# A SwiGLU layer on one core: the second quarter-chunk of x is loaded by rows and transposed by TensorE

## The chip, the core and the metric

The kernel runs on one core of one Trainium2 chip. The metric is the device time of one execution in microseconds. The kernel before takes 115.9 us, the median of three runs (115.56, 115.90 and 116.58).

## The reference

```
B, S, D, F = 1, 2048, 512, 1376          # all bf16
def reference(x, w_gate, w_up, w_down):
    g = silu(x @ w_gate)                 # (S, D) @ (D, F)
    u = x @ w_up
    return (g * u) @ w_down              # (S, F) @ (F, D)
```

## The kernel before, in words

The product of gate and up wants D, the contracted dimension, on the partitions, so x is held transposed in `xT_sb` (128 partitions, KD = 4 blocks of D, 2048 tokens). Tokens come in four chunks of 512 (`SC`). Half of the first chunk, `HT` = 256 tokens, is a unit of its own in this change. The weights of gate and up come in slabs of two feature tiles of 128 (`wg0`, `wu0`, then `wg2`, `wu2` and so on) into `w_sb`; w_down comes later into `wd_sb`.

The program is a list of operations (`Plan`). TensorE (P) and SyncE (S, which issues the loads) run theirs in the order in which they were added. ScalarE (A), VectorE (D) and GpSimd (G) get theirs from `schedule`, which takes at each step the operation that could start first by a table of estimated durations and landing times (`land`), and at equal starts the one with the lower priority number. `emit` then puts in the semaphore waits. Operations that read a key wait for its last writer; those that write one wait for its readers too. A key `("b", i)` is PSUM bank i.

The loads in order on SyncE's queue: `xn` (tokens 0 to 255, by rows: partition p holds tokens 2p and 2p + 1), `wg0`, `x0b` (tokens 256 to 511 by a transposing DMA, `load_x`, straight into `xT_sb`), `wu0`, the slab 2 of gate and of up, `x1a` and `x1b` (tokens 512 to 1023, transposing), slabs 4 and 8, `x2`, `x3`, slab 6, w_down and its pieces.

TensorE's start: `warm` (6 matmuls of 512 columns and 2 small ones on constants), then the transposes of `xn` by a product with `ident`, for each of the four blocks dk of D: for dk 0 to 2 four transposes of 64 x 64-row pieces into two banks (L373), for dk 3 four half-width ones into bank 6 (L380). After each dk the piece is copied from PSUM to `xT_sb` (`copy_op`), dk 0 and 2 by VectorE (L326), dk 1 and 3 by ScalarE (L325). Then `between`: N_BETWEEN = 5 pairs of small matmuls on constants into bank 7 (L397), whose result nobody reads. Then the gates of feature tiles 0 and 1 (L424 through `gu_emit`): first on columns 0 to 255, dk by dk as the copies come, then on columns 256 to 511, which wait for `x0b`. Then the ups of both tiles on all 512 columns, which wait for `wu0`. These use pairs of 64-column matmuls side by side in the array.

Behind that, in TensorE's fixed order: feature tiles 2 and 3 of chunk 0, three feature tiles of chunk 1 (all still L424), the products for the last 96 features (`plan_x` L488, `plan_y` L514), and then the main part: Strassen-Winograd units (seven products in place of eight on 2 x 2 blocks) in fp32 for gate and up, whose operands are sums that GpSimd builds from the weights (`w_sums`) and VectorE or GpSimd from x (`x_sums`). The down product is made in part in the same way, in part directly (L720, L748, L858, L870).

Loading by rows leaves the tokens of `xn` in another order in `xT_sb` (position 128 i + p holds token 2p + i). The order is undone where the output is stored: `put` stores tokens 0 to 255 (`fa`) with the pattern `(p j) d` and the rest of chunk 0 with `(j p) d`.

The lines the change touches around the gates are

```
for dk in range(KD):
    for ft, b in ((0, g0), (1, g1)):
        pe(gu_emit(0, ft, 0, b, [dk], 0, HT), [("x0a", dk), wkey[0]], [("b", b)], 0.5)
for ft, b in ((0, g0), (1, g1)):
    pe(gu_emit(0, ft, 0, b, range(KD), HT, SC), ["x0b", wkey[0]], [("b", b)], 2)
```

Of the kernel before, what the change touches and what calls it, by code (L numbers as in the profile page):

```python
# [6 lines left out]
BF16 = mybir.dt.bfloat16  # L7
# [2 lines left out]

N_WARM = 6
N_FILL = 1
N_BETWEEN = 5

PE_STEP, PE_STEP4, PE_LAG = 216, 231, 205
A_BUSY, A_LAG = 485, 180
# [152 lines left out]
def bass_standalone__swiglu_ffn__prompt_kernel(nc, x, w_gate, w_up, w_down, out):  # L169
    _, S, D = x.shape  # L170
    F = w_gate.shape[1]
    P = 128
    KD = D // P
# [4 lines left out]
    SC = 512  # L178
    NSC = S // SC
    TPC = SC // P  # L180
# [4 lines left out]
    HT = SC // 2  # L185
    HC = P // 2
    NXN = HT // P
    NB = 8
# [4 lines left out]
    xf = x[0]  # L193
    of = out[0]
# [4 lines left out]
    with ExitStack() as es:  # L199
        sb = lambda name, shape, dt: es.enter_context(nc.sbuf_tensor(name, shape, dt))  # L200
# [3 lines left out]
        xT_sb = sb("xT_sb", [P, KD, S], BF16)  # L204
# [22 lines left out]
        psum = ps("psum", [P, NB, 512], FP32)  # L227
        turn = [0, 2, 1, 3, 4, 5, 6, 7]
        bank = lambda i: psum[:, i, :]

        xn_sb = sb("xn_sb", [P, NXN, D], BF16)
        ident = sb("ident", [P, P], BF16)
        diag = sb("diag", [P, P], mybir.dt.int32)

# [6 lines left out]
            rest.remove(i)  # L241
            return i

        homes = dict(xn=14, x0b=22, wg0=30, x0c=13, wu0=21, wg2=29, wu2=20, wg4=12, wu4=28, wg6=19)

        ones_w = nc.const_aps.tensor(1.0, [P, P], BF16)
        ones_m = nc.const_aps.tensor(1.0, [P, SC], BF16)
# [29 lines left out]
        def load_x(name, t0, t1):  # L277
            load(
                name, lambda e: e.dma_start_transpose(xT_sb[:, :, t0:t1], xf[t0:t1, :]), [name], 1500, 4 * (t1 - t0)  # L279
            )  # L280

        load(
            "xn",
            lambda e: e.dma_start(  # L284
                xn_sb[:, :, :].rearrange("p j d -> p (j d)"), xf[0:HT, :].rearrange("(p j) d -> p (j d)", j=NXN)
            ),
            ["xn"], 500, 770,
        )
# [33 lines left out]
        def copy_op(engs, out, src, reads, writes, prio, busy=None, after=()):  # L322
            def emit(e):
                if e is engines["A"]:
                    return e.activation(out, src, ACT.Copy)  # L325
                return e.tensor_copy(out, src)  # L326
            b = A_BUSY if engs == "A" else D_BUSY
            return plan.add(engs, emit, reads, writes, busy or b, A_LAG if engs == "A" else D_LAG, prio, after=after)
# [16 lines left out]
        def pe(emit, reads, writes, n, step=PE_STEP, after=()):  # L345
            return plan.add("P", emit, reads, writes, int(n * step), PE_LAG, dma=None, after=after)
# [17 lines left out]
        def tview_last():  # L364
            return psum[:, 6, 0:P].bitcast(BF16).rearrange("p (i t) -> p i t", i=NXN)

        def transposes(dk):
            def emit(e):
                for i in range(NXN):
                    if dk < KD - 1:  # L370
                        for h in range(2):
                            t0 = h * HC
                            ins = e.transpose(  # L373
                                tview(dk)[:, h, i, :], xn_sb[t0:t0 + HC, i, dk * P:(dk + 1) * P],
                                ident[t0:t0 + HC, t0:t0 + HC],
                            )
                    else:
                        for m in (0, HC):
                            c0 = dk * P + m
                            ins = e.transpose(tview_last()[m:m + HC, i, :], xn_sb[:, i, c0:c0 + HC], ident[:, :])  # L380
                return ins
            return emit

        for dk in range(KD):
            keys = [("b", 2 * dk), ("b", 2 * dk + 1)] if dk < KD - 1 else [("b", 6)]
            pe(transposes(dk), ["xn", "ident"], keys, 0.5)
            out, src = xT_sb[:, dk, 0:HT], tview_last()
            if dk < KD - 1:
                out, src = out.rearrange("p (i h t) -> p h i t", i=NXN, h=2), tview(dk)
            else:  # L390
                out = out.rearrange("p (i t) -> p i t", i=NXN)
            copy_op("DA"[dk % 2], out, src, keys, [("x0a", dk)], 0, 300)

        def between(e):
            for i in range(N_BETWEEN):
# [4 lines left out]
                    )  # L400
            return ins

        pe(between, (), [("b", NB - 1)], N_BETWEEN / 4)

        n_group = 0

# [6 lines left out]
        def x_keys(c):  # L413
            if c == 1:
                return ["x1a", "x1b"]
            if c:
                return [f"x{c}"]
            return [("x0a", dk) for dk in range(KD)] + ["x0b"]

        def gu_emit(m, ft, c, b, dks, n0, n1):  # L420
            def emit(e):
                for dk in dks:
                    for h in (0, HC):
                        ins = e.matmul(  # L424
                            psum[h:h + HC, b, n0:n1], lhsT=w_sb[:, dk, m, ft * P + h:ft * P + h + HC],
                            rhs=xT_sb[:, dk, c * SC + n0:c * SC + n1], start=(dk == 0), stop=(dk == KD - 1),
                            tile_position=(0, h),
                        )
                return ins
            return emit  # L430
# [417 lines left out]
        class DownUnit:  # L848
# [82 lines left out]
            def put(self, c):  # L931
                d0 = 2 * self.q
                reads = [("fin", d, c) for d in (d0, d0 + 1)]
                c0, c1 = d0 * P, (d0 + 2) * P
                if c == 0:
                    store(f"fa{d0}", "A", of[0:HT, c0:c1].rearrange("(p j) d -> p j d", j=NXN), fin_sb[:, 0:NXN, c0:c1], reads)
                t0 = NXN if c == 0 else TPC
                t1 = (c + 1) * TPC
                store(f"f{c}{d0}", "A", of[t0 * P:t1 * P, c0:c1].rearrange("(j p) d -> p j d", p=P), fin_sb[:, t0:t1, c0:c1], reads)

        def last_rest(c0, c1, b):
            t, ob = LAST_T, LAST_T - NST // 2
# [144 lines left out]
```

## Time and profile before

| | us |
|---|---|
| median of three runs (lowest to highest) | 115.9 (115.56 to 116.58) |
| the profiled execution, its own time | 115.87 |
| its span in the profile | 114.5 |
| TensorE matmul busy | 110.8 (97%) |
| VectorE busy | 76.8 (67%) |
| ScalarE busy | 63.7 (56%) |
| GpSimd busy | 61.5 (54%) |
| HBM read | 4.75 MB |

The profile shows one execution. PE is TensorE's matmuls, PEld its weight loads, DVE VectorE, ACT ScalarE, POOL GpSimd, SPq SyncE's queue, where a row's length is the time to issue a DMA, not to move it. L with a number is a line of the kernel. In a row of the timeline the first number is the start from the beginning of the span, the second the length, in us; x with a number counts instructions, and the bracket gives the idle time before and what ended it. Matmul ends are modelled and contain the way through the array, so neighbouring matmuls overlap in their rows, and their rate is read from their starts.

### The profile page before, as it was taken

What the parts mean: (1) busy time and instruction counts of PE and PEld (TensorE: products, weight loads), DVE (VectorE), ACT (ScalarE), POOL (GpSimd) and SP (SyncE); (2) the same over time, 40 slices, a digit from 0 to 9 for tenths busy, and PEclk for the clock granted to TensorE, in tenths of its full rate; (3) what the DMA queues carried; (4) which work ended last, traced back from release to release, by engine and by line L of the source; (5) the groups of instructions that cost most, each with busy time, mean ns of one, the idle gap of its engine ahead of it and who ended that gap; (6) DMA issues with size and microseconds to landing.
All of it is one profiled execution on the core that took longest, in us unless ns stands there. A gap on an engine that the chain in (4) does not pass through costs nothing.

```text
span 114.5 us, 1775 instructions
## 1 busy us (share of the span) xinstructions
PE 110.8 (97%) x652; PEld 69.6 (61%) x660; DVE 76.8 (67%) x113; ACT 63.7 (56%) x123; POOL 61.5 (54%) x57
## 2 busy tenths in 40 slices
PE   7999999999999999999999999999999999999993
PEld 2755566556675857677676858654344557866452
DVE  0113999783966849493958768499999957486423
ACT  5344665865779897767678786740567960000000
POOL 1049103999999999977999989965000000000000
DMA  3999999994000000000000000000031002227876
GB/s 88 265 242 219 325 210 220 273 370 100 0 0 0 3 0 3 0 0 6 0 0 0 3 0 0 0 0 0 13 130 46 0 0 46 52 46 183 195 202 199
DMA packets 22808, 9.84 MB, mean 86 GB/s; under 512 B 12848, under 2 KB 22672, under 8 KB 22800
## 3 DMA queue, kind: packets, MB, share of 16 engines
q1 hardware_dynamic: 20656, 8.69, 31.5%
q10 hardware_dynamic: 2144, 1.05, 3.3%
q8 instruction: 5, 0.08, 0.3%
q14 instruction: 3, 0.02, 0.1%
HBM read 4.75 MB, written 2.10 MB: 60 GB/s over the span
## 4 chain that ended last, share of the span: by engine, by line
PE 91%; DMA 4%; SPq 2%; issue 1%; DVE 1%
PE psum L610 32%; PE psum L720 15%; PE psum L622 12%; PE psum L858 10%; PE psum L424 9%; PE psum L870 4%; DMA w_sb<-in_w_up_dram 4%; PE psum L488 3%; PE psum L748 3%; PE psum L435 2%; PE psum L514 2%; SPq L279 1%; DVE o_sb L326 1%; SPq L267 0%; SPq L284 0%
## 5 line engine op out<-in xcount | busy, mean ns | idle before, releaser
L610 PE MATMUL psum<-tt_sb,ss_sb 128*128 128x512 f32 x160 | 40.1, 404 | 0.0
L610 PEld LDWEIGHTS psum<-tt_sb,ss_sb 128*128 128x128 f32 x160 | 29.9, 188 | 7.6 <-DVE h_sb L337 0.3
L337 DVE TENSOR_TENSOR ts_sb<-r_sb,psum 128x512 f32<-128x512 f32 x32 | 20.6, 681 | 14.8 <-ACT r_sb L325 14.8
L337 POOL TENSOR_TENSOR h_sb<-sg_sb,ts_sb 128x512 bf16<-128x512 f32 x16 | 20.8, 1301 | 2.9 <-ACT sg_sb L332 2.9
L337 DVE TENSOR_TENSOR h_sb<-sg_sb,psum 128x512 bf16<-128x512 f32 x24 | 16.4, 682 | 6.2 <-PE psum L424 5.8
L325 ACT ACTIVATE r_sb<-psum 128x512 f32<-128x512 f32 x32 | 17.3, 596 | 5.5 <-PE psum L610 5.5
L332 ACT ACTIVATE sg_sb<-psum 128x512 f32<-128x512 f32 x24 | 14.3, 600 | 10.6 <-PE psum L610 5.4
L337 POOL TENSOR_TENSOR ss_sb<-w_sb 128x512 fp32r<-128x512 bf16 x10 | 11.4, 1159 | 13.6 <-DVE tt_sb L337 7.1
L720 PE MATMUL psum<-wd_sb,h_sb 128*128 128x512 bf16 (+2 forms) x98 | 17.9, 336 | 0.2 <-issue 0.2
L622 PE MATMUL psum<-xT_sb,w_sb 128*128 128x512 bf16 x59 | 14.2, 380 | 0.4 <-issue 0.2
L720 PEld LDWEIGHTS psum<-wd_sb,h_sb 128*128 128x128 bf16 x100 | 8.2, 98 | 9.2 <-issue 1.0
L424 PE MATMUL psum<-xT_sb,w_sb 128*64 128x512 bf16 (+1 forms) x128 | 12.7, 354 | 0.2 <-DMA w_sb<-in_w_up_dram 0.2
L332 ACT ACTIVATE sg_sb<-ts_sb 128x512 f32<-128x512 f32 x16 | 10.2, 636 | 2.3 <-DVE ts_sb L337 2.3
L424 PEld LDWEIGHTS psum<-xT_sb,w_sb 128*64 128x64 bf16 x128 | 7.7, 112 | 4.8 <-DMA w_sb<-in_w_up_dram 0.5
L622 PEld LDWEIGHTS psum<-xT_sb,w_sb 128*128 128x128 bf16 x64 | 5.5, 98 | 8.0 <-issue 2.5
L326 DVE COPY psum<-psum 128x512 f32<-128x512 f32 x8 | 5.6, 699 | 0.8 <-PE psum L622 0.2
L337 POOL TENSOR_TENSOR ss_sb<-w_sb,ss_sb 128x512 fp32r<-128x512 bf16 x5 | 5.8, 1169 | 0.2
L337 POOL TENSOR_TENSOR ss_sb<-ss_sb,w_sb 128x512 fp32r<-128x512 f32 x5 | 5.8, 1165 | 0.0
L326 DVE CAST o_sb<-psum 128x512 bf16<-128x512 f32 (+2 forms) x6 | 2.9, 512 | 4.2 <-PE psum L720 3.1
L337 POOL TENSOR_TENSOR ss_sb<-wd_sb 128x640 fp32r<-128x640 bf16 x4 | 5.6, 1409 | 0.0
L858 PE MATMUL psum<-tt_sb,ss_sb 128*128 128x512 f32 x20 | 5.6, 417 | 0.0
L858 PE MATMUL psum<-th_sb,ss_sb 128*128 128x512 f32 x20 | 5.5, 413 | 0.0
(72 smaller groups left out, 122.3 us busy)
## 6 DMA issues: line engine op xcount, KB each, us to landing
wd_sb<-in_w_down_dram SPq DMA_DIRECT2D x1, 1280.0 KB, 8.3
w_sb<-in_w_gate_dram SPq DMA_DIRECT2D x4, 256.0 KB, 4.0
w_sb<-in_w_up_dram SPq DMA_DIRECT2D x4, 256.0 KB, 4.2
out_dram<-o_sb SPq DMA_DIRECT2D x7, 128.0 KB, 1.8
out_dram<-xT_sb ACTq DMA_DIRECT2D x4, 128.0 KB, 2.3
out_dram<-xT_sb ACTq DMA_DIRECT2D x2, 256.0 KB, 3.3
w_sb<-in_w_gate_dram SPq DMA_DIRECT2D x1, 352.0 KB, 5.0
w_sb<-in_w_up_dram SPq DMA_DIRECT2D x1, 320.0 KB, 5.5
```

The source lines that it names most:

```text
L325: return e.activation(out, src, ACT.Copy)
L326: return e.tensor_copy(out, src)
L332: "A", lambda e: e.activation(out, src, ACT.Silu), reads, writes, busy, A_LAG, prio
L337: engs, lambda e: e.tensor_tensor(out, a, b, alu), reads, writes, busy,
L424: ins = e.matmul(psum[h:h + HC, b, n0:n1], lhsT=w_sb[:, dk, m, ft * P + h:ft * P + h + HC], rhs=xT_sb[:, dk, c * SC + n0:c * SC + n1], sta ...
L488: ins = e.matmul(psum[m:m + HC, b, :], lhsT=w_sb[:, dk, 0, XC0 + m:XC0 + m + HC], rhs=xT_sb[:, dk, c * SC:(c + 1) * SC], start=(dk == 0), ...
L610: ins = e.matmul(bank(dst), lhsT=s[:, k, :], rhs=t[:, k, :], start=(start and k == 0), stop=(k == KH - 1), skip_group_check=True,)
L622: ins = e.matmul(bank(dst), lhsT=w_sb[:, k0 + k, m, f:f + P], rhs=xT_sb[:, k0 + k, c:c + SC], start=(start and k == 0), stop=(k == KH - 1) ...
L720: ins = e.matmul(psum[:, b, 0:c1 - c0], lhsT=hrows(F_ORDER[n], t, 0, P), rhs=wd_sb[:, F_ORDER[n], c0:c1], start=(start and n == n0), stop= ...
L748: ins = e.matmul(bank(b), lhsT=lhsT, rhs=rhs, start=(start and n == 0), stop=(n == 2 and (kind == "T" or not start)), tile_position=(r0, 0 ...
L858: ins = e.matmul(bank(dst), lhsT=self.ds[s][:, j, self.q, :], rhs=self.dt[t][:, j, :], start=(start and n == 0), stop=(n == NFF // 2 - 1), ...
L870: ins = e.matmul(bank(dst), lhsT=wd_sb[:, 2 * j + a, d * P:(d + 1) * P], rhs=h0_sb[:, 2 * j + a, 0:SC], start=(n == 0), stop=(n == NFF // ...
```

## The change

Tokens 256 to 511 are no longer loaded by the transposing DMA `x0b` but by rows into a second tile, `xn1`, issued as the second load, right behind `xn0` (the old `xn`). TensorE transposes them as it does the first 256: 16 more transposes, four more copies (two on VectorE, two on ScalarE), the last block into bank 7 in place of 6. `between` moves between the two halves and has 3 pairs in place of 5. The gates of tiles 0 and 1 run on all 512 columns at once, dk by dk, and wait for the copies of both halves. The stores of chunk 0 use the pattern `(p j) d` for both halves.

```
-N_BETWEEN = 5
+N_BETWEEN = 3
...
-        xn_sb = sb("xn_sb", [P, NXN, D], BF16)
+        xn_sb = [sb(f"xn_sb{i}", [P, NXN, D], BF16) for i in range(2)]
...
+        def load_xn(i):
+            load(
+                f"xn{i}",
+                lambda e: e.dma_start(
+                    xn_sb[i][:, :, :].rearrange("p j d -> p (j d)"),
+                    xf[i * HT:(i + 1) * HT, :].rearrange("(p j) d -> p (j d)", j=NXN),
+                ),
+                [f"xn{i}"], 500, 770,
+            )
+
+        load_xn(0)
+        load_xn(1)
         load_w("wg0", w_gate, 0, 0, 0, slabs[0][1] * P)
-        load_x("x0b", HT, SC)
         load_w("wu0", w_up, 1, 0, 0, slabs[0][1] * P)
...
+        for half, last in enumerate((6, 7)):
+            if half:
+                pe(between, (), [("b", NB - 1)], N_BETWEEN / 4)
+            for dk in range(KD):
+                keys = [("b", 2 * dk), ("b", 2 * dk + 1)] if dk < KD - 1 else [("b", last)]
+                pe(transposes(half, dk, last), [f"xn{half}", "ident"], keys, 0.5)
+                out, src = xT_sb[:, dk, half * HT:(half + 1) * HT], tview_last(last)
...
+                copy_op("DA"[dk % 2], out, src, keys, [("x0", half, dk)], 0, 300)
...
         for dk in range(KD):
             for ft, b in ((0, g0), (1, g1)):
-                pe(gu_emit(0, ft, 0, b, [dk], 0, HT), [("x0a", dk), wkey[0]], [("b", b)], 0.5)
-        for ft, b in ((0, g0), (1, g1)):
-            pe(gu_emit(0, ft, 0, b, range(KD), HT, SC), ["x0b", wkey[0]], [("b", b)], 2)
+                pe(gu_emit(0, ft, 0, b, [dk], 0, SC), [("x0", 0, dk), ("x0", 1, dk), wkey[0]], [("b", b)], 1)
...
                 if c == 0:
-                    store(f"fa{d0}", "A", of[0:HT, c0:c1].rearrange("(p j) d -> p j d", j=NXN), fin_sb[:, 0:NXN, c0:c1], reads)
...
+                    for i in range(2):
+                        store(
+                            f"f{i}a{d0}", "A", of[i * HT:(i + 1) * HT, c0:c1].rearrange("(p j) d -> p j d", j=NXN),
+                            fin_sb[:, i * NXN:(i + 1) * NXN, c0:c1], reads,
+                        )
```

More of the change, by code (lines that the diff above doesn't have):

```diff
@@ L242, in take @@
             return i
-        homes = dict(xn=14, x0b=22, wg0=30, x0c=13, wu0=21, wg2=29, wu2=20, wg4=12, wu4=28, wg6=19)
+        homes = dict(xn0=14, xn1=22, wg0=30, x0c=13, wu0=21, wg2=29, wu2=20, wg4=12, wu4=28, wg6=19)
         ones_w = nc.const_aps.tensor(1.0, [P, P], BF16)
@@ L362, in tview, with tview_last, transposes @@
             return psum[:, 2 * dk:2 * dk + 2, 0:HC].bitcast(BF16).rearrange("p h (i t) -> p h i t", i=NXN)
-        def tview_last():
-            return psum[:, 6, 0:P].bitcast(BF16).rearrange("p (i t) -> p i t", i=NXN)
-        def transposes(dk):
+        def tview_last(b):
+            return psum[:, b, 0:P].bitcast(BF16).rearrange("p (i t) -> p i t", i=NXN)
+        def transposes(half, dk, last):
             def emit(e):
@@ L373, in emit @@
                             ins = e.transpose(
[L374 removed]
+                                tview(dk)[:, h, i, :], xn_sb[half][t0:t0 + HC, i, dk * P:(dk + 1) * P],
                                 ident[t0:t0 + HC, t0:t0 + HC],
@@ L379, in emit @@
                             c0 = dk * P + m
-                            ins = e.transpose(tview_last()[m:m + HC, i, :], xn_sb[:, i, c0:c0 + HC], ident[:, :])
+                            ins = e.transpose(tview_last(last)[m:m + HC, i, :], xn_sb[half][:, i, c0:c0 + HC], ident[:, :])
                 return ins
             return emit
[L384 to L392, printed above, removed]
         def between(e):
@@ L417, in x_keys @@
                 return [f"x{c}"]
-            return [("x0a", dk) for dk in range(KD)] + ["x0b"]
+            return [("x0", half, dk) for half in range(2) for dk in range(KD)]
         def gu_emit(m, ft, c, b, dks, n0, n1):
```

17 lines of the change are left out of this document (6 added, 11 removed).

## The prediction

> **What bounds the kernel now.** I read the chain of work that ended last first, by line and in order of time, because its pieces say which engine every microsecond of the end depends on.
>
> ```profile
> span 114.5 us, 1775 instructions
> PE 91%; DMA 4%; SPq 2%; issue 1%; DVE 1%
> 1.67 1.33 SPq L279
> ...
> 3.04 4.01 DMA w_sb<-in_w_up_dram
> 7.05 0.04 issue
> 7.10 10.71 PE psum L424 x96
> 17.80 1.73 PE psum L488 x16
> ...
> 104.92 6.82 PE psum L720 x34
> 111.74 0.18 PE psum L945
> ```
>
> From 7.10 us to 111.9 the chain is TensorE almost without a break; ahead of it stand SP's issues and the landing of the first up slab (wu0) at 3.04 + 4.01 = 7.05. So whatever lets the up groups start earlier comes off the end one for one, and nothing else does unless it removes a gap from TensorE's row. One quantity to carry along: 16 matmuls of 64 columns on 512 take 1.73, so 0.108 each, 0.216 a pair.
>
> Second, the start in order of time, TensorE and the two engines that copy out of PSUM. The columns are start, length, engine, line, what, count.
>
> ```profile
> 0.77 2.72 PE L350 MATMUL psum<-const-bfloat16-1.0 128*128 128x512 bf16 x6 [0.77 <-PEq L1072]
> 3.71 0.50 PE L373 MATMUL psum<-ident,xn_sb 64*128 64x64 bf16 x12
> 4.14 0.43 PE L380 MATMUL psum<-ident,xn_sb 128*64 128x128 bf16 x4
> 4.35 0.75 PE L397 MATMUL psum<-const-bfloat16-1.0 128*64 128x128 bf16 x10
> 4.88 1.98 PE L424 MATMUL psum<-xT_sb,w_sb 128*64 128x256 bf16 x32
> 7.10 10.71 PE L424 MATMUL psum<-xT_sb,w_sb 128*64 128x512 bf16 x96 [0.23 <-DMA w_sb<-in_w_up_dram]
> 4.03 0.51 DVE L326 COPY xT_sb<-psum 128x256 bf16<-128x256 bf16 x2 [2.71 <-PE psum L373]
> 4.14 0.85 ACT L325 ACTIVATE xT_sb<-psum 128x256 bf16<-128x256 bf16 x2 [1.91 <-PE psum L373]
> ```
>
> A length ends with a pipeline tail, so I reckon in starts. Transposes of one half: 3.71 to 4.35, **0.64**. Filler: ten matmuls from 4.35 to 4.88, so 0.106 a pair. Gates: 16 pairs of 256 columns from 4.88, at 0.110 a pair (half of 0.216 and a little), leave the array free at 6.64; the ups come at 7.10. Here lie **0.46 us** in which TensorE could take work (the profile calls 0.23 of it idle, the rest is the tail of the last matmuls).
>
> Third, the transfers: SP's issues, and the time from issue to landing of each by windows around its issue.
>
> ```profile
> 0.74 0.40 SPq L284 DMA_DIRECT2D xn_sb<-in_x_dram  x1
> 1.21 0.41 SPq L267 DMA_DIRECT2D w_sb<-in_w_gate_dram  x1
> 1.67 1.33 SPq L279 DMA_TRANSPOSE xT_sb<-in_x_dram  x1
> 3.04 0.57 SPq L267 DMA_DIRECT2D w_sb<-in_w_up_dram  x1
> 7.24 1.51 SPq L279 DMA_TRANSPOSE xT_sb<-in_x_dram  x1
> xn_sb<-in_x_dram SPq DMA_DIRECT2D x1, 256.0 KB, 2.8
> w_sb<-in_w_gate_dram SPq DMA_DIRECT2D x1, 256.0 KB, 3.2
> xT_sb<-in_x_dram SPq DMA_TRANSPOSE x1, 3.9
> xT_sb<-in_x_dram SPq DMA_TRANSPOSE x1, 5.1
> ```
>
> xn lands at 0.74 + 2.8 = 3.54, wg0 at 1.21 + 3.2 = 4.41, x0b (the transposing load, 3.9) at 5.57, wu0 at 7.05. The row with 5.1 is x1b, the second half of tokens 512-1023, issued at 7.24: it lands at 12.34.
>
> **The change part by part.**
>
> *SP's queue.* The 1.33 us issue of x0b goes, a plain load of x by rows (xn1) takes its place one position further forward, at the 0.40 of xn. Issues: xn0 0.74, xn1 1.21, wg0 1.67, wu0 2.14, and so 3.04 - 2.14 = 0.90 earlier for wu0 and for everything behind it (second slabs, x1a, x1b, and on).
>
> *Landings.* xn0 as now, 3.54. xn1 stands where wg0 stood, has its 256 KB, and comes in rows of 2 KB in place of pieces of 512 B, so 4.41 is its upper end; the lower is xn0's own, 3.54, as the two are neighbours. I take 4.41, as no row shows a transfer in second place sooner. For wg0, now third, the ends are 4.41 (its old place) and 5.57 (the third place as x0b had it). The gap from the first to the second landing was 4.41 - 3.54 = 0.87 for a plain transfer of this size, so I take 4.41 + 0.87 = 5.28. wu0 likewise 5.28 + 0.87 = 6.15, with the ends 5.57 (x0b's old landing, which it can at best replace at third place) and 7.05.
>
> [...]
>
> *TensorE before the gates.* Same start: first transposes 3.71 to 4.35. Then the filler, three pairs in place of five: 3 x 0.106 = 0.32, to 4.67. Then the second half's transposes, another 0.64, to 5.31. Three things could hold these up. xn1 is there at 4.41, covered by the filler by 0.26; at its upper end still covered. They write the banks that the first half's copies read: DVE's two are through at 4.03 + 0.51 = 4.54, the first of ACT's at about 4.14 + 0.39 = 4.53, all ahead of 4.67; the last group has a bank of its own, 7, which only the filler uses. Without the filler as cover the copies would be what they wait for. Queued behind a late transpose would be every gate, and so the whole chain.
>
> ```profile
> L326 DVE COPY xT_sb<-psum x2: 292/292/292, 4.0 to 4.2; 128x256 bf16<-128x256 bf16 x2
> L325 ACT ACTIVATE xT_sb<-psum x2: 384/384/385, 4.1 to 4.6; 128x256 bf16<-128x256 bf16 x2
> ```
>
> *Copies.* Two more on DVE, two more on ACT. The first copy began 4.03 - 3.71 = 0.32 behind the first transpose, and DVE takes 0.29 for each. So x of the second half, first 128 dims, is ready at 4.67 + 0.32 + 0.29 = 5.28, and with the 0.05 that wu0 shows between landing (7.05) and use (7.10) the first gate can start at **5.34**, just behind the last transpose (5.31) and wg0 (5.28 + 0.05). ACT is the slower of the two: its two copies take 0.39 each and 0.85 together. The next two follow behind 4.99 and the transposes, at about 5.13 and 5.59, and end at 5.52 and 5.98. The second dk step of the gates is due at 5.34 + 2 x 0.216 = 5.77, the fourth at 6.64. Covered by 0.25 and 0.66; if ACT ran half a microsecond late the gates would lose about 0.25.
>
> *Gates on 512 columns.* 16 matmuls at 0.108 = 1.73, in place of 16 pairs at 0.110 = 1.76: only 0.03 cheaper in array time. What is new is that the first gate needs both halves. It starts 0.46 later than the present 4.88. End: 5.34 + 1.73 = **7.07**. wu0 has been there since 6.15 (at its upper end, 7.05, too), so it no longer decides. The ups start at 7.07 against 7.10: **-0.03**. That is the heart of it: the 0.46 us gap is filled, but by 0.64 of transposes less 0.21 of filler.
>
> *Behind it.* One gap is left in the first 96 up and gate matmuls.
>
> ```profile
> 12.43 0.62 PE L424 MATMUL psum<-xT_sb,w_sb 128*64 128x512 bf16 x4
> 12.38 0.63 ACT L541 ACTIVATE tt_sb<-xT_sb 128x512 fp32r<-128x512 bf16 x1 [1.01 <-DMA xT_sb<-in_x_dram]
> ```
>
> The groups on tokens 512-1023 come after 24 pairs, 7.10 + 24 x 0.216 = 12.29, but start at 12.43, just behind x1b at 12.34: **0.14** lost. With x1b issued 0.90 earlier it lands at about 11.44, and TensorE wants it at 12.26. The gap goes, -0.14; if x1b were bound by the engines' bandwidth and came no earlier it stays (0). What is next due are x2 and x3, also 0.90 earlier for a need that moves by 0.17. DVE's sums of x1 begin sooner and may change places with a product of the first chunk, which frees bank 6, needed only by the first tail group (L488 in the chain, 17.80 now); I cost that at nothing. The output stores are as many and as large as before, and those of chunk 0 go out while TensorE still has down matmuls to do.
>
> *Sum.* The profiled execution took 115.87 us, 1.37 more than its span of 114.5, close to the median of the runs, 115.90. -0.03 - 0.14 = -0.17: **115.7 us**. Bounds from the open costs: with wg0 at its lower end, and filler and second transposes at twice their present rate, the gates come up to (0.32 + 0.64) / 2 = 0.48 sooner, 115.2; with wg0 at 5.57 the first gate comes at 5.62, 0.28 later, 116.0, and another 0.14 if x1b comes no sooner either, though the later start then hides it. All of it lies within 1%, which is about what a measurement of this kernel can tell from no change.
>
> **The rivals.**
>
> *The array is still at half rate when the gates come (slower).* The rows of the matmuls show how long one takes, in ns, along the start:
>
> ```profile
> L350 PE MATMUL psum<-const-bfloat16-1.0 128*128 128x512 bf16 x6 | 2.7, 626 | 0.8 <-PEq L1072 0.8
> L397 PE MATMUL psum<-const-bfloat16-1.0 128*64 128x128 bf16 x10 | 0.7, 314 | 0.0
> L424 PE MATMUL psum<-xT_sb,w_sb x32: 272/273/341, 4.9 to 6.6; 128*64 128x256 bf16 x32
> ```
>
> The six opening matmuls start (2.72 - 0.63) / 5 = 0.42 apart, twice the 0.216 of later ones. 128-column filler takes 314 ns, yet the 256-column gates 273 in the median with the slowest at 341: full rate came with the first gates, 4.88 - 0.77 = 4.1 us after TensorE began. The change takes two dense filler pairs from just ahead of that point and puts sparse 64-column transposes there. Should that keep the half rate, or should a wait for xn1 or a copy open a hole, the gates would take 8 x 0.42 = 3.36 rather than 1.73 and the sum would be 115.7 + 1.63 = **117.3**. Up to there the price is half the time from 5.34 to the turn, so it eats the gain from a turn at 5.7 on and makes the kernel slower by over 1% from one at 8.0. For it: before, the 0.46 gap would absorb the first part of such a delay, after it nothing does, and the three runs shown lie 1.0 apart (115.56 to 116.58), as a turn at varying times would leave them. Against it: TensorE's row is as full up to 4.67 as now. [...]
>
> *wu0's landing stays the bound (faster).* If the transposes ran wholly in the shade, the ups would start with wu0 at 6.15 + 0.05 = 6.20: -0.90 - 0.14, **114.8**, and with wu0 at its lower end 114.3. Against it: 0.32 + 0.64 + 1.73 = 2.69 of TensorE work after 4.35 ends at 7.04, and fits ahead of 6.20 only if nearly all of it but the gates is gone.
>
> *The transfers gain nothing.* wg0 comes at 5.57 as x0b did, x1b at 12.34: gates 5.62 to 7.35, ups +0.25, and the later start swallows the x1b gap (-0.14): **116.0**. For it, the 16 DMA engines' share in 40 slices of 2.9 us, near full from the second to the ninth:
>
> ```profile
> DMA  3999999994000000000000000000031002227876
> ```
>
> **How the numbers follow.** Forecast 115.7: 0.47. Transfers gain nothing, 116.0: 0.10. Half rate through the gates, 116.5 to 117.5: 0.31. wu0 the bound, 114.3 to 114.8: 0.12. The first two stay within 1%; of the slow rival 0.04 stays below 117.06 and of the fast one 0.02 above 114.74: same 0.63, slower 0.27, faster 0.10. The likeliest one's own range is 115.2 to 116.1. For eight in ten I leave out most of the fast rival and the slow one's far end: **115.0 to 117.3**.
>
> **What would show it.** Right: SP issues wu0 near 2.1; 24 transposes on 64 rows and 8 on 128, ending near 5.3; first gate near 5.3, 16 of them on 512 columns at 0.108; ups near 7.07 without a wait on wu0; no gap near 12.3; the rest of TensorE's row unchanged, only shifted by 0.2. Wrong: a first gate after 5.7 (a late landing or copy; the waits name it), gate matmuls of over 600 ns (half rate), ups before 6.6, or a new gap between 17 and 26 where the order of DVE's work has moved.

## The result and the profile after

The changed kernel takes 116.64 us in the median of 22 runs, the kernel before 115.90 in the median of 22 runs on the same chip. The ratio is 1.0059, 95% interval 1.0040 to 1.0078: slower by 0.74 us, where 0.2 us less had been forecast. Three of the 22 runs of the changed kernel came out at 118.9 to 119.1; ratios, here and below, leave out such runs, over 1.5% above the fastest of the same kernel.

The chain of work that ended last, its head and its end, in the profiled execution of the changed kernel (117.13 us, span 115.8; columns: start, length, what):

```profile
span 115.8 us, 1772 instructions
PE 91%; DMA 4%; issue 1%; DVE 1%; SPq 1%
1.66 4.48 DMA w_sb<-in_w_gate_dram
...
6.28 12.28 PE psum L429 x112
18.55 1.73 PE psum L493 x16
...
105.80 6.82 PE psum L723 x34
112.62 0.18 PE psum L951
```

Before, the chain's head was wu0, which landed at 7.05 and let the ups start at 7.10, behind gates that were done. Now it is wg0, and the first gate waits for it until 6.28. All 112 gate and up matmuls follow without a gap, where 96 of the old 128 followed at 7.10 with a gap of 0.14. The same start in order of time, from SP's issues to the first gate:

```profile
0.74 0.87 SPq L285 DMA_DIRECT2D xn_sb<-in_x_dram  x2
1.66 0.43 SPq L267 DMA_DIRECT2D w_sb<-in_w_gate_dram  x1
2.13 0.51 SPq L267 DMA_DIRECT2D w_sb<-in_w_up_dram  x1
3.81 4.42 SPq L279 DMA_TRANSPOSE xT_sb<-in_x_dram  x2
3.62 0.50 PE L377 MATMUL psum<-ident,xn_sb 64*128 64x64 bf16 x12
...
4.57 0.35 PE L377 MATMUL psum<-ident,xn_sb 64*128 64x64 bf16 x12
4.84 0.30 PE L384 MATMUL psum<-ident,xn_sb 128*64 128x128 bf16 x4
4.84 0.49 DVE L330 COPY xT_sb<-psum 128x256 bf16<-128x256 bf16 x2 [0.39 <-PE psum L377]
6.28 3.00 PE L429 MATMUL psum<-xT_sb,w_sb 128*64 128x512 bf16 x26 [1.13 <-DMA w_sb<-in_w_gate_dram]
```

The issues stand where they were forecast (wu0 at 2.13), the second transposes run from 4.57 to about 5.1, the copies follow, and then TensorE idles 1.13 us for wg0.

The end differs too. SP issues seven transpositions of results there, from 93.6 us on before and from 94.5 on after. The first row is the fourth of them, the second the fifth, the third VectorE's final copies; first the kernel before, then the changed one:

```profile
102.45 1.19 SPq L897 DMA_TRANSPOSE xT_sb<-xT_sb  x1
103.68 1.32 SPq L897 DMA_TRANSPOSE xT_sb<-xT_sb  x1
111.94 0.87 DVE L326 CAST o_sb<-psum 128x384 bf16<-128x384 f32 x3 [1.10 <-PE psum L945]
```

```profile
103.33 1.75 SPq L900 DMA_TRANSPOSE xT_sb<-xT_sb  x1
105.12 1.52 SPq L900 DMA_TRANSPOSE xT_sb<-xT_sb  x1
112.82 0.88 DVE L330 CAST o_sb<-psum 128x384 bf16<-128x384 f32 x3 [1.10 <-PE psum L951]
```

From the last copy's end to the end of the span it was 114.5 - 112.81 = 1.69 and is 115.8 - 113.70 = 2.10. (A span is given to 0.1 us, so a tail is good to about 0.05.) The two transpositions hold SP 0.76 longer and the end comes 0.41 later behind the last copy; that the one makes the other, through the output stores queued behind, is read from their order and not shown by a run.

### The profile page after: what moved, and what is told of

It reads as the page before. It is cut to its first block, busy times and chain, and to the rows that moved or that the text cites. A ratio compares the mean times of both kernels' runs of the same rounds, so it can differ in the third digit from the quotient of the medians.

```text
span 115.8 us, 1772 instructions
## 1 busy us (share of the span) xinstructions
PE 110.8 (96%) x648; PEld 69.8 (60%) x656; DVE 77.2 (67%) x115; ACT 64.6 (56%) x125; POOL 61.5 (53%) x57
## 4 chain that ended last, share of the span: by engine, by line
PE 91%; DMA 4%; issue 1%; DVE 1%; SPq 1%
PE psum L615 32%; PE psum L723 14%; PE psum L627 12%; PE psum L429 11%; PE psum L861 10%; DMA w_sb<-in_w_gate_dram 4%; PE psum L873 4%; PE psum L493 3%; PE psum L751 3%; PE psum L519 1%; PE psum L440 1%; DVE o_sb L330 1%; SPq L285 1%; PE psum L951 0%
## 5 line engine op out<-in xcount | busy, mean ns | idle before, releaser
L429 PE MATMUL psum<-xT_sb,w_sb 128*64 128x512 bf16 x112 | 12.3, 379 | 1.1 <-DMA w_sb<-in_w_gate_dram 1.1
```

What stands on the lines that cost most here:

```text
L429: ins = e.matmul(psum[h:h + HC, b, n0:n1], lhsT=w_sb[:, dk, m, ft * P + h:ft * P + h + HC], rhs=xT_sb[:, dk, c * SC + n0:c * SC + n1], sta ...
```

## The experiments

All kernels but where it is said otherwise are the changed kernel with the edit shown. A list at the end of a load's arguments names the loads that must have landed before SyncE issues it. A time without a ratio is that of one execution.

### What delays wg0

**Hold everything behind wg0 until it has landed.**

```
-load_w("wu0", w_up, 1, 0, 0, slabs[0][1] * P)
+load_w("wu0", w_up, 1, 0, 0, slabs[0][1] * P, ["wg0"])
```

> The changed kernel, but SyncE issues wu0 and everything behind it only once wg0 has landed. So nothing follows wg0 on the way. Theory S (transfers in flight share the engines, and what is issued behind wg0 stretches it): wg0 lands at 5.1 to 5.5 in place of 6.14, the first gate comes at 5.3 to 5.6. Theory P (wg0 is late because of its place behind 512 KB and its small pieces alone): wg0 still lands at 6.0 to 6.2. In both wu0 is then issued late and lands some 2.5 to 3 us behind wg0, so the ups wait for it and the whole is slower than the changed kernel: 117.5 to 118.5 by S, 118 to 119 by P.

118.52 us. The chain of waits:

```profile
1.66 3.64 DMA w_sb<-in_w_gate_dram
```

wg0 lands at 5.30, next to the 5.28 of the prediction, and the first gate starts at 5.44. The price is wu0: the ups wait 0.98 for it, to 8.34, and x1b comes later too.

**Hold only what lies behind wu0.**

```
-load_slab(*slabs[1])
+load_slab(*slabs[1], ["wg0"])
```

> The changed kernel, but SyncE issues only what stands behind wu0 (slab 2 and on) after wg0 has landed; wu0 is issued at 2.1 as in the changed kernel. Theory S with the sharing among all that is in flight: wg0 at 5.4 to 5.8, between the kernel with everything held and the changed one; if wu0 alone does the stretching, still 6.1. Theory P: 6.0 to 6.2. The slabs behind come some 3 us later than in the changed kernel and x1 with them, so a gap opens ahead of the groups on tokens 512 to 1023: 117 to 119 in all.

117.5 us. wg0 lands at 1.66 + 3.81 = 5.47, the gates start at 5.61, the ups don't wait. But x1b was issued late, and the groups on tokens 512 to 1023 wait for it:

```profile
5.61 7.13 PE L430 MATMUL psum<-xT_sb,w_sb 128*64 128x512 bf16 x64
13.54 0.84 PE L430 MATMUL psum<-xT_sb,w_sb 128*64 128x512 bf16 x6 [0.80 <-DMA xT_sb<-in_x_dram]
```

In these two executions wg0 came 0.7 to 0.8 sooner than in the first of the changed kernel, and the hold was paid for at the ups or at x1b. How far wg0's landing varies without a hold is told below.

**Hold wu0 and all behind until xn1 has landed.**

```
-load_w("wu0", w_up, 1, 0, 0, slabs[0][1] * P)
+load_w("wu0", w_up, 1, 0, 0, slabs[0][1] * P, ["xn1"])
```

> The changed kernel, but SyncE issues wu0 and all behind it only once xn1 has landed (4.2). Theory S1 and S2: nothing but wg0 is under way until 4.2, and the transposing loads come from 6 us on, so wg0 lands at 5.2 to 5.4 and the first gate comes near 5.45. wu0, issued at 4.25 and without a transposing load beside it, lands at 7.0 to 7.4, the ups start at 7.2 to 7.4, and x1b lands some 2 us later than in the changed kernel, near 12.8 to 13.2, a gap of 0.3 to 0.7 ahead of its groups: 116.3 to 116.8. Theory P (place and piece size): wg0 5.9 to 6.1, 117 and more.

116.99 us, ratio 1.0087 (1.0059 to 1.0114). wg0 at 1.66 + 3.7 = 5.4, gates at 5.53; the 112 matmuls take 12.90 in place of 12.28, and not for a wait: the rows of the matmuls have 634 ns from 5.5 to 6.0 and 379 from 6.8 on, so the array turned to full rate near 6.7.

**Hold x1a, the transposing load, and all behind it until wg0 has landed.**

```
-    load_x(f"x1{'ab'[i]}", SC + i * HT, SC + (i + 1) * HT)
+    load_x(f"x1{'ab'[i]}", SC + i * HT, SC + (i + 1) * HT, [] if i else ["wg0"])
```

> The changed kernel, but SyncE issues the transposing load x1a (and all behind it) only once wg0 has landed; wu0 and slab 2 go out as in the changed kernel. In the packets of the profiles so far, 512-byte pieces move at 145 to 170 per quarter of a microsecond, and at 105 to 140 while SyncE is busy issuing a transposing load. Theory S1 (the transposing load, whose issue the change moved from 4.76 to 3.81 and so on top of wg0, is what slows it): wg0 lands at 5.3 to 5.6. Theory S2 (any transfer queued behind wg0 slows it, plain ones as much): 5.8 to 6.1 as in the changed kernel. By S1 the first gate comes near 5.6, the ups near 7.3, and x1b, issued some 1.5 us later than in the changed kernel, lands near 12.5 and is just in time or leaves a gap of some tenths: 116.1 to 116.5. By S2 116.6 to 117.0.

116.62 us, ratio 1.0064 (1.0042 to 1.0086), the profiled execution at 116.01. In that one the chain runs through the copies and not through wg0, as the prediction had it for the whole kernel:

```profile
4.81 0.50 DVE xT_sb L331 x2
...
5.31 12.28 PE psum L430 x112
```

I read this at first as proof that the issue of the transposing load, on top of wg0 from 3.81 on, is what delays it. A second execution of the same kernel took that back.

> The version that holds x1a until wg0 has landed, unchanged, once more. Theory of the landing alone: wg0 5.1 to 5.3, first gate 5.3 to 5.5, matmuls at full rate, tail 1.7 to 2.1, a time of 116.0 to 116.4 that follows from these. Theory of the late turn: wg0 as early, but the 112 matmuls from the first gate on take 12.5 to 13 in place of 12.28, and the time comes out near the median of 116.6 by just that. Theory of the tail: matmuls at 12.28, tail over 2.1.

116.68 us, and wg0 as late as without the hold:

```profile
1.66 4.08 DMA w_sb<-in_w_gate_dram
...
5.87 12.28 PE psum L430 x112
```

The transposing load was issued only at 5.75 here. It is not needed for the delay.

**Leave xn1 out.** Both halves are transposed from the first 256 tokens, so the results of tokens 256 to 511 are those of other tokens.

```
-load_xn(1)
...
-tview(dk)[:, h, i, :], xn_sb[half][t0:t0 + HC, i, dk * P:(dk + 1) * P],
+tview(dk)[:, h, i, :], xn_sb[0][t0:t0 + HC, i, dk * P:(dk + 1) * P],
...
-pe(transposes(half, dk, last), [f"xn{half}", "ident"], keys, 0.5)
+pe(transposes(half, dk, last), ["xn0", "ident"], keys, 0.5)
```

> The changed kernel without the load of xn1: both halves are transposed from the first 256 tokens, so the results of tokens 256 to 511 are those of other tokens. wg0 is second on the queue as before the change, but wu0 is issued 1.4 us sooner behind it than there (at 1.7 in place of 3.04). Theory P: wg0 lands at 4.4 to 4.6, as before the change. Theory S: later than before the change, 4.8 to 5.3. The first gate is then bound by transposes and copies at about 5.2 to 5.4, as the prediction had it, wu0 lands at 5.5 to 6.2, ups at 7.0 to 7.1, total 115.6 to 115.8 by both.

116.31 us. wg0, now second in the queue, lands at 4.3, and the first gate starts at 5.41, right behind the transposes. So the second position gives 4.3, as before (4.4); it is the third that is dear. The time did not come down to 115.6 to 115.8 as expected: the array ran at half rate until about 5.9 (607 to 636 ns for the matmuls of 5.4, 379 for most of those from 5.8 on; 17.74 - 5.41 = 12.33 from the first gate to the group behind the 112, against 18.36 - 6.28 = 12.08 in the changed kernel's first profile), and the tail was 2.1.

**wg0 second, xn1 third.**

```
 load_xn(0)
-load_xn(1)
 load_w("wg0", w_gate, 0, 0, 0, slabs[0][1] * P)
+load_xn(1)
```

> The changed kernel with one edit: wg0 is loaded second and xn1 third. wg0 lands at 4.4 to 4.8 by both theories. Theory P: xn1, in large rows, lands about 0.7 behind it, at 5.1 to 5.3, and the first gate comes 0.80 later (transpose, copy, hand-over), at 5.9 to 6.1: ups at 7.6 to 7.8, total 116.2 to 116.5. Theory S: xn1 is stretched by wu0 and the slabs issued behind it, 5.6 to 6.0, first gate 6.4 to 6.8: total 116.8 to 117.2, no better than the changed kernel.

118.62 us in the median of five, ratio 1.0232 (1.0213 to 1.0251), more than either theory gave. The third position is dear for xn1 just as for wg0, though its rows are 2 KB. The profiled execution took 120.81:

```profile
1.67 4.94 DMA xn_sb<-in_x_dram
...
6.74 0.51 PE psum L377 x12
...
7.60 14.79 PE psum L429 x112
```

The hole in TensorE's row is 2 us long, and in this execution the 112 matmuls behind it take 14.79 in place of 12.28 without a wait in the chain; that this is half rate is read from the sum alone. The loss, 2.51, is more than the 2.2 by which this execution lies above the median. So the median has the late first gate without the loss, as far as the sum tells.

### The pattern of the stores

**The old pattern in the changed kernel** (the order of tokens 256 to 511 is not undone), and **the new pattern in the kernel before** (it disorders the tokens that the old pattern leaves in order).

```
-for i in range(2):                                      # changed kernel
+for i, how in enumerate(("(p j) d -> p j d", "(j p) d -> p j d")):
...
-of[i * HT:(i + 1) * HT, c0:c1].rearrange("(p j) d -> p j d", j=NXN),
+of[i * HT:(i + 1) * HT, c0:c1].rearrange(how, j=NXN),
...
-store(f"f{c}{d0}", "A", of[t0 * P:t1 * P, c0:c1].rearrange("(j p) d -> p j d", p=P), fin_sb[:, t0:t1, c0:c1], reads)   # kernel before
+how = "(p j) d -> p j d" if c == 0 else "(j p) d -> p j d"
+store(f"f{c}{d0}", "A", of[t0 * P:t1 * P, c0:c1].rearrange(how, p=P), fin_sb[:, t0:t1, c0:c1], reads)
```

> The changed kernel, but the results of tokens 256 to 511 are stored with the old pattern, so their order is not undone and those rows go to other tokens' places. It asks where the 0.4 us come from by which the changed kernel's last store ends later than TensorE's delay explains. Theory T1 (the new store pattern is slower to issue and collides with the transposing DMAs at the end): the tail shrinks back, ACT's six stores take about 8.6 us in place of 9.9, and the kernel is 0.3 to 0.5 faster than the changed one, ratio to before about 1.002 to 1.003. Theory T2 (only the moment at which the stores fall): no difference, ratio 1.006.

> The kernel before the change with nothing but the new store pattern on tokens 256 to 511 (their rows go to other places). Theory T1 (the pattern is slower): ACT's six stores take about 9.9 us in place of 8.6, the last store lands 0.3 to 0.5 later, ratio 1.003 to 1.004. Theory T2 (only the moment): as before, ratio 1.000 within 0.001.

The first has a ratio of 1.0033 (1.0001 to 1.0066), with eight of its twelve runs at 115.9 to 117.0 and four at 118.3 to 120.4 (median 116.82), and a tail of 1.83; the second takes 116.1, ratio 1.0006 (0.9986 to 1.0025), with the tail of before, 1.69. In the kernel before the pattern costs nothing that shows. In the changed kernel the old one leaves the fourth transposition long (1.73) but has the fifth at 1.27 in place of 1.52, and the tail between the two. So the pattern alone doesn't lengthen the tail, but a part of it, some 0.25, may hang on the two together: one execution shows it, and the intervals of the ratios overlap.

**One more transposing load**, of 256 tokens, at the end of the loads, since the changed kernel issues one fewer and its later transpositions on SP come out longer:

```
+late = xn_sb[1][:, :, :].rearrange("p j d -> p (j d)").rearrange("p (k t) -> p k t", k=KD)
+load("xlate", lambda e: e.dma_start_transpose(late, xf[HT:SC, :]), ["xn1"], 1500, 4 * HT)
```

> The changed kernel plus one transposing load of 256 tokens, the size of the removed x0b, issued at the end of all loads, near 24 us, into a tile that is no longer read. It asks why the 4th and 5th of the transposing DMAs of the output take 1.75 and 1.52 us to issue in every kernel derived from the changed one, while in the kernel before the long ones are the 2nd or 3rd, and the last store ends 0.35 us later. Theory Q (the long issue falls at a certain count of packets on the queue, which the removed load shifted): the long issue moves back to the 2nd or 3rd, the last store lands 1.7 us behind the last copy in place of 2.1, 0.3 to 0.4 faster than the changed kernel, ratio 1.002 to 1.003. Theory R (it is not the count): as the changed kernel, ratio 1.006.

Ratio 1.0068 (1.0036 to 1.0101): six of its twelve runs took 116.1 to 117.4 and six 118.2 to 118.9 (median 117.82). In the profiled execution (116.07) the tail is back at 1.65 and none of the first five transpositions takes more than 1.3. But the next kernel, which has no more loads than the changed one, has a tail of 1.7 too, and the ratio didn't fall to the 1.002 to 1.003 that theory Q gave. So the extra load isn't shown to be what shortens the tail.

### The rate of the array

**Ten pairs of filler between the second transposes and the gates**, so that TensorE does not idle while it waits for wg0:

```
+pe(waiting, (), [("b", 6)], 10 / 4)       # 20 matmuls of 128 columns into bank 6
```

> The changed kernel plus ten pairs of 128-column filler matmuls behind the second half's transposes, so that TensorE has about 1.07 us of work at half rate while it waits for wg0; the gates start at the landing of wg0 or at the filler's end, 6.2, whichever is later. Theory C (the hole in TensorE's work delays the moment at which the array goes to full rate, as the second profile of the changed kernel shows, where the 112 first gate and up matmuls took 13.9 us in place of 12.3): the highest executions, 118 to 119 for the changed kernel, no longer occur, and the median stays within 0.2 of the changed kernel's, 116.4 to 116.8. Without C: the same spread as the changed kernel, 116.2 to 119.

116.56 us, ratio 1.0063 (1.0041 to 1.0085), the highest of 8 runs at 117.09. In the profiled one (117.01) wg0 landed at 5.7 and the gates waited for the filler, to 6.35; by an estimate from the time to the next group, 18.66 - 6.35 = 12.31 against 12.08, the array was at half rate until some 0.4 us after that; the tail was 1.7. None of the 8 runs came near 119, but with 3 of 22 of the changed kernel doing so, 8 without one would be no surprise.

**The kernel before with wu0 ahead of x0b, and the ups of the first 256 columns ahead of the gates of the second 256.** It packs TensorE in another way, without more transposes.

```
+load_w("wu0", w_up, 1, 0, 0, slabs[0][1] * P)
 load_x("x0b", HT, SC)
-load_w("wu0", w_up, 1, 0, 0, slabs[0][1] * P)
...
-for ft, b in ((0, g0), (1, g1)):
-    pe(gu_emit(0, ft, 0, b, range(KD), HT, SC), ["x0b", wkey[0]], [("b", b)], 2)
 for ft, b in ((0, u0), (1, u1)):
-    gu_group(1, ft, 0, b)
+    pe(gu_emit(1, ft, 0, b, range(KD), 0, HT), [("x0a", dk) for dk in range(KD)] + [wkey[1]], [("b", b)], 2)
+for m, bs in ((0, (g0, g1)), (1, (u0, u1))):
+    for ft, b in enumerate(bs):
+        pe(gu_emit(m, ft, 0, b, range(KD), HT, SC), ["x0b", wkey[m]], [("b", b)], 2)
```

> The kernel before the change, with wu0 loaded ahead of x0b and the ups on the first 256 columns made ahead of the gates on the second 256, so that the work that needs x0b comes last; no transposes are added. Theory S (transfers in flight share the engines, so a third transfer lands late): wu0, third on the queue and issued at 1.67, lands at 5.4 to 6.2, and x0b, fourth, at 6.5 to 7.2. The gates on 256 columns end at 5.76 as before, the ups on 256 columns run from about 6.0 to 6.9, and the rest from about 7.0, all done by 8.8 as before the change: 115.7 to 116.1, no gain. Theory P (place and piece size alone): wu0 at 5.3, x0b at 6.4, TensorE without a gap from 4.88, the four groups done at 8.4 rather than 8.83: 115.4 to 115.6.

115.87 us, ratio 0.9997 (0.9976 to 1.0018). wu0, a plain load in third place, landed at 1.67 + 3.9 = 5.57. In the profiled execution (116.21) TensorE is dense from the first gate on, as the chain of waits shows:

```profile
5.11 12.99 PE psum L424 x144
18.10 1.73 PE psum L488 x16
```

but the array is at half rate until about 6.8, as the groups of 256-column matmuls from 5.5 on, from 6.5 on and from 7.0 on show (minimum, median and maximum ns of one):

```profile
L424 PE MATMUL psum<-xT_sb,w_sb x10: 421/421/422, 5.5 to 6.4; 128*64 128x256 bf16 x10
L424 PE MATMUL psum<-xT_sb,w_sb x10: 272/346/421, 6.2 to 6.9; 128*64 128x256 bf16 x10
L424 PE MATMUL psum<-xT_sb,w_sb x16: 272/272/273, 6.8 to 7.6; 128*64 128x256 bf16 x16
```

The same work takes 18.36 - 6.28 = 12.08 in the changed kernel's first profile, from the first gate to the start of the next group, and 17.93 - 4.90 = 13.03 here. Nearly all of the 0.95 more is half rate, and it outweighs the 0.60 that filling the gaps of 0.46 and 0.14 could give. The profiled execution is 0.34 above the median, which none shows.

### More executions of both kernels

The profiled execution of the changed kernel (117.13) is not its median. Three more of it, unchanged, and one of the kernel before:

> The changed kernel as it is, for a second profile: how far the landing of wg0 moves from one execution to the next. Theory S and P alike: 5.8 to 6.2 (6.14 in the first profile), first gate 5.9 to 6.3; the execution's time moves with it one for one, 116.4 to 117.1.

> The changed kernel, unchanged, a third look. Theory of the landing: wg0 5.6 to 6.2, first gate 0.15 behind it, 112 matmuls in 12.28, and the time is 116.6 or so with the tail at 1.7 to 2.1. Theory of the late turn: the 112 matmuls take 12.5 or more. One of the three terms has to vary by what the times vary.

> The changed kernel, unchanged, a fourth look; the same expectations as for the third: wg0 5.6 to 6.2; then either 112 matmuls in 12.28 and the end follows the landing, or more than 12.5 and it follows the rate; tail 1.7 to 2.1.

> The kernel before, unchanged, once more. Theory of the landing: wu0 7.05, ups 7.10, last copy of VectorE ends at 112.8, tail 1.7. If wu0 comes later, as the 7.49 of the version with only the new store pattern showed, the ups go with it, and the gap ahead of x1b (0.14) shrinks by as much. If the tail shows 2.0 or more here, then it isn't the change that lengthens it.

The first gates came within what was expected, the times did not: the second missed its 116.4 to 117.1 by the half rate, the third by a late x1b, which had not been among its theories. Of the kernel before, the ups were expected at 7.10 and came at 6.8.

| execution | us | first gate | lost behind it | last copy ends | tail |
|---|---|---|---|---|---|
| changed, first | 117.13 | 6.28 | 0 | 113.70 | 2.10 |
| changed, second | 118.47 | 6.00 | 1.62 half rate | 115.05 | 2.05 |
| changed, third | 117.53 | 5.86 | 0.78 x1b | 114.14 | 2.06 |
| changed, fourth | 118.42 | 5.90 | 1.71 half rate | 115.05 | 2.05 |
| x1a held, first | 116.01 | 5.31 | 0 | 112.76 | 1.94 |
| x1a held, second | 116.68 | 5.87 | 0 | 113.30 | 2.10 |

The loss at half rate is what the 112 matmuls took less 12.28. That by x1b is the start of its groups, 13.55, less the first gate and 64 matmuls at 0.108. Last copy less first gate less loss is 107.42 to 107.50 in all six: between the start and the last copy nothing else varies. The kernel before has tails of 1.69 and, in the second (116.22 us), 114.9 - 113.20 = 1.70; there wu0 was early enough (6.7), and x1b cost 0.61. So what bounds the start varied in the kernel before, too, and the prediction had it from one execution.

The fourth shows a late turn. Its gate and up matmuls from 8.5 on, those up to 9.3 and, for comparison, those from 8.5 on of the third (minimum, median and maximum ns of one, then the stretch):

```profile
L429 PE MATMUL psum<-xT_sb,w_sb x6: 634/634/634, 8.0 to 8.9; 128*64 128x512 bf16 x6
L429 PE MATMUL psum<-xT_sb,w_sb x6: 431/634/634, 8.4 to 9.3; 128*64 128x512 bf16 x6
```

```profile
L429 PE MATMUL psum<-xT_sb,w_sb x8: 378/379/380, 8.2 to 8.9; 128*64 128x512 bf16 x8
```

634 ns is the half rate, 379 the full one; the granted clock that the profile lists reads 1.00 throughout, so only the matmuls' own rows show the difference. In the fourth the second transposes still ran slowly and the gates started 0.40 behind them at half rate:

```profile
5.08 0.43 PE L384 MATMUL psum<-ident,xn_sb 128*64 128x128 bf16 x4
5.90 3.63 PE L429 MATMUL psum<-xT_sb,w_sb 128*64 128x512 bf16 x16 [0.40 <-DMA w_sb<-in_w_gate_dram]
5.90 13.99 PE psum L429 x112
```

The third has the last four transposes at full rate (0.30 long) and then a wait for x1b:

```profile
5.00 0.30 PE L384 MATMUL psum<-ident,xn_sb 128*64 128x128 bf16 x4
5.86 7.10 PE L429 MATMUL psum<-xT_sb,w_sb 128*64 128x512 bf16 x64 [0.55 <-DMA w_sb<-in_w_gate_dram]
6.57 6.85 DMA xT_sb<-in_x_dram
13.55 4.94 PE L429 MATMUL psum<-xT_sb,w_sb 128*64 128x512 bf16 x44 [0.60 <-DMA xT_sb<-in_x_dram]
```

x1b took 6.85 from its issue, against 5.1 in the prediction's row, although it was issued at 6.57 and not at 7.24.

## Why the prediction was wrong, point by point

**The step that failed is the landing of wg0.** The prediction said: "I take 4.41 + 0.87 = 5.28", with 5.57 as the upper end. Four executions had the first gate at 5.86 to 6.28, 0.14 behind wg0 (0.05 had been taken from wu0), so wg0 at 5.7 to 6.14, beyond the upper end. The increment of 0.87 from one landing to the next was read from the first and second transfers, and carried over to the third. With nothing issued behind wg0 the landing came as forecast (5.30), 1.1 behind xn1 at 4.20, and nearly so with wu0 held until xn1 has landed (5.4, 1.2 behind it). In the changed kernel wu0 and the second slabs are issued while wg0 moves. Without a hold wg0 also landed at about 5.4, 5.7 and 6.0 (in the versions with one more load at the end, with more filler, and with the old stores), so the spread of one place is as large as what the holds change. The chip is not separated from it either: chip 3 gave 5.2 and 5.4 with a hold and 5.4 and 5.7 without, chip 12 gave 5.7 with and 5.7 and 5.8 without.

The upper end was no bound: x0b's 5.57 came from one execution, x0b itself landed at 5.3 and 5.8 in two others of the old order, and wg0 was later than 5.57 in all four. Nor do the rows of before show that a plain load lands sooner than x0b did: its 3.9 from issue to landing stands there beside 2.8 and 3.2 of plain loads, but those stood in first and second place; a plain load in third place took 3.9 (wu0 with the ups first) and 4.1 to 4.5 (wg0 in the four).

What the DMA view shows of wg0's delay is the start of the third transfer. In the 0.75 us from 3.5 on the changed kernel moves 199 packets in its first profile (236 to 314 in the other three), the version with nothing behind wg0 403 (the line counts all packets; those under 2 KB are nearly all pieces of weights):

```profile
DMA packets 199, 0.11 MB, mean 151 GB/s; under 512 B 8, under 2 KB 189, under 8 KB 199
```

```profile
DMA packets 403, 0.22 MB, mean 296 GB/s; under 512 B 15, under 2 KB 388, under 8 KB 403
```

Why it starts slowly is open. The transposing load is not needed for it, as the second execution with x1a held shows (255 packets). That plain transfers queued behind are what does it fits the two executions that held them, but two against such a spread don't show it.

**A second step, put at nothing, is the end.** "The output stores are as many and as large as before": they are, and the tail still went from 1.7 to between 2.05 and 2.10 in all four executions. SP's fourth transposition takes 1.73 to 1.77 there in place of 1.19, the fifth 1.52 in place of 1.28 to 1.32. The store pattern alone is not the cause (1.69 in the kernel before), though it may have a part together with the long fourth; the extra load settles nothing. What makes the fourth long stays open. Not tried: a version that changes only when ScalarE issues its stores.

**The sum with the measured terms.** The prediction's sum stands on its gates at 5.34. In the first profile the first gate came 6.28 - 5.34 = 0.94 later, 0.86 of it the landing; the tail adds 0.41, and a further 0.12 was not forecast: the third long unit of the main part takes 4.78 to 4.81 in the four in place of 4.65 to 4.66 (at 43.85 and 43.09 in the two first profiles). It too has no known cause. 115.7 + 0.94 + 0.41 + 0.12 = 117.17, and that execution took 117.13.

```profile
43.85 4.78 PE psum L615 x20
```

```profile
43.09 4.66 PE psum L610 x20
```

No execution at the median, 116.64, was profiled. By the same sum it has its first gate near 5.8, a little ahead of the earliest of the four; that is inferred.

The median lies inside the stated range, 115.0 to 117.3, by luck: the likeliest account's own bounds end at 116.1, and the range goes higher for the half rate, which the sum of the median doesn't need. The rival by which the transfers gain nothing (116.0) had the right place and sign for wg0, but fell short there. On x1b it was wrong: in three of the four x1b landed at 10.3 to 10.4, sooner than forecast (11.44), and in the third at 13.42, later than before (12.34).

**The half-rate rival is real, but it is not the median.** It was given 117.3 and 0.31. It happened in two of the four, which took 118.4 to 118.5: the gates started at 5.9 to 6.0, and full rate came at 5.90 + 2 x 1.71 = 9.3 and 6.00 + 2 x 1.62 = 9.2. Other kernels turned at 5.9 (xn1 left out), near 6.7 (wu0 held, and more filler) and 6.8 (ups first), so a turn also comes at times between. Its price, half the time to the turn, is right: in the fourth the rows of the matmuls turn near 9.3, as the sum has it. The two lost 1.71 and 1.62, next to the 1.63 in the prediction's 117.3. With the gates at 7.5 in the order with wg0 second, 14.79 - 12.28 = 2.51 lost puts the turn at 12.5 by an estimate at the same price. What sets the moment of the turn no run shows. The runs at 119 may be of this kind, but none of those was profiled. That the hole ahead of the gates brings it about is not borne out: the second and fourth had slow transposes before the hole opened, and their hole, 0.40, is shorter than those of executions that had the full rate from the first gate on (1.13 in the first, 0.55 in the third, 0.61 with the old stores, whose transposes were slow, too).

**What was right, but for small things.** wu0 is issued at 2.13 (2.14 forecast). The transposes end at 5.1 (5.31), with VectorE's first copy of the second half at 4.84 (4.99). 16 gates on 512 columns run at 0.108 each when the rate is full. wu0 no longer decides (it lands at 6.5 to 6.9, not at 6.15, and is needed from 7.6 on), and x1b's gap of 0.14 goes in three of the four. x1b is issued only 0.37 to 0.67 sooner, not 0.90, because the issue of x1a takes 2.7 to 3.0 (2.44 before). The second transposes fill the old gap, so even with everything in time little was to be had: the held version's profiled execution, with wg0 in time, is at 116.01 against 115.87, its gates 0.03 earlier than forecast, and loses by the tail and the long unit what the start gains.

**What the prediction saw only for the rate, and not for the landing,** is that nothing behind the gates absorbs a delay any more. Before, wu0 was needed only at 6.64, and what came late in the gates was absorbed by the 0.46 gap behind them. Now wg0 is behind one more transfer of 256 KB and is needed by the first gate, so its delay reaches the end one for one: in six executions the last copy follows the first gate by the same 107.4 to 107.5 once the other losses are taken off.

No version here beats the kernel before; the one with the ups of the first columns ahead equals it.

## What to carry to other kernels

Moving a transfer one place back in the queue had no fixed price here: in the four executions of the changed kernel the third 256 KB landed 1.6 to 2.0 us after the second (xn1 at 4.1 to 4.2), where 0.87 had been read off the first and second, and the landing moved by 0.4 us between executions. When a change makes the first matmul need one transfer more, price its landing by the latest row of a transfer at that place with as much queued behind it, or leave the range open upwards. And profile more than one execution before a median is explained by a profile: here a late slab, a late x1b and a late full rate took turns in the same program.

## What the runs showed of the hardware that was not expected

- The same program, four times: wg0 landed over 0.4 us, x1b took no time or 0.78, and full rate came before the gates or 3.3 us behind their start.
- A transfer's place counted for more than its rows: third in the queue, xn1 with rows of 2 KB took 4.94 from issue to landing (one execution), wg0 with pieces of 512 B 3.8 to 4.5 without a hold; second in the queue, xn1 took 2.8 to 3.0 and wg0 3.1 to 3.5.
- With later transfers held back wg0 landed at 5.2 to 5.5 in four of five executions (5.7 in the other), against 5.4 to 6.1 in the seven without a hold. Where the hold was strict it cost as much or more at the next one needed: the ups waited 0.98, or x1b's groups 0.80.
- Of the first four transpositions that SP issues late in the kernel, one takes 1.6 to 2.1 in place of 1.2 in most executions. Where it is the second or third, the tail stays at 1.7; where it is the fourth, the tail is 0.25 to 0.45 longer (0.14 in the version with the old store pattern).
- A plain load of 256 KB in third place (wu0 with the ups first) took 3.9 from issue to landing, and a transposing one of 256 tokens there 3.6 to 4.1; what differed was the issue, 1.3 against 0.4 to 0.5.
